# Moving a convolution's transposes from TensorE to DMA, and reordering the second row half, in a fused H3 and feed-forward kernel

## The chip, the cores and the metric

The kernel runs on one core of a Trainium2 chip, in one launch. The metric is the time of an execution in microseconds on the device, the median of several runs. A profile of one execution, taken by the hardware profiler, gives the durations.

## The reference, cut to what matters

The inputs are `q`, `k`, `v` and `x` of 2048 rows by 1024 channels; only `q` is used as x. The output is x plus a gated long convolution plus a feed-forward layer, both on the layer norm of x.

```python
xn = layernorm(q)
# long convolution, channel by channel
k_shift = sum of 4 taps of k           # causal, depthwise
kv = k_shift * v
y = irfft(rfft(kv padded to 2S) * rfft(ssm_k padded to 2S))[:S] + kv * ssm_D
conv = xn * y
# feed-forward
ffn = silu(xn @ w1) @ w2               # 1024 -> 3584 -> 1024
out = q + conv + ffn
```

## The kernel before, in words

**Precision and matmuls.** Every large operand is split into a high and a low fp16 part (`split`, L357: ACT writes the high part, then DVE writes the rest, `lo = src * scale - hi`). A product of 128 x 128 by 128 x 512 is then three matmuls (high by high, high by low, low by high).

**Feed-forward.** GEMM1 (lines L921 to L997) makes the hidden layer, transposed. The 28 column blocks of `w1` are taken as 14 pairs and the 2048 rows as two halves. Pairs 0 and 1 of the first half are plain. All the rest go as `units` (L962): a unit is one pair by one row half, done by seven products P1 to P7 of twelve matmuls each (a Strassen-Winograd scheme), each with its own left factor (B11, T1 and so on, in the `wo` buffers, made by `factors_w1`, L745) and its own moving operand (A11, S1 and so on, in the `x` places). The order is pairs 2 to 13 on the first half, then 0 to 13 on the second. In a unit the products stand as P7, P6, P2, P5, then P1 of the next unit, P3, P4, with PSUM banks evacuated by ACT and DVE (`evacuate`, L889).

Factors of pairs 2 to 13 are made once, used in the first half, written to DRAM (`spill_w1`, L786) and read back for the second half (`load_factors`, L797); pairs 0 and 1 are made for the second half alone, at the end of the first. The second half's seven moving operands lie in DRAM and come by seven transposing DMAs of 1 MB (`load_x`, L999; `X`, L326), each as soon as the first half's last unit has freed the place.

GEMM2 multiplies the hidden layer, written to DRAM and read back, by `w2`. The four pairs named in `PAIRS` (L43, 10 to 13) use the seven-product scheme again: their hidden values are combined and spilled by `quad` (L809) into `hsf`; the others are spilled by `blocks` (L851) into `hs`. Both write through two buffers `ht`.

**Convolution.** Eight groups g of 128 channels. `gate` (L1385) computes the taps and the product with v into `acc`, channels on partitions. `signal_parts` (L1436) prepares the transform's input for four parts t in the order 1, 3, 0, 2: TensorE transposes four 128 x 128 blocks of `acc` (fp32, against an identity) into the PSUM bank `px` (L1451), ACT and DVE split `px` into the first half of `hi` and `lo`; the filter `kf`, which comes from DRAM with time on partitions already, is split into the second half. `stage1` (L1459) multiplies by DFT constants, twelve matmuls per half part into PSUM banks `ps`. `to_spec` (L1496) moves sums and differences into `spec` and `tmp`. `forward` (L1511) does the butterflies on DVE, after all four parts; `product`, `inverse`, `result_parts` and `stage1_inv` (L1664, bank `py`) follow. `gated` (L1686) multiplies `py` by the normed rows `xg` into `yt`, and POOL adds `yt` to the output in DRAM (`G`, L331). Scales come from small matmuls (`norm`, L426) in the `px` bank.

**What sets the order.** All work is written as generators (streams), and `Order.run` (L165) takes, step by step, the operation that could start first by the kernel's own table of costs less a bias of its stream. The result is a fixed order on each engine and on SP's queue, which issues nearly all DMAs; each engine keeps its order and waits on semaphores. Ring buffers (L263) decide when a stream may go on.

Names on the engines in the profile: PE (TensorE), DVE (VectorE), ACT (ScalarE), POOL (GpSimd), SP (queue SPq). `split` shows as L347 (ACT) and L339 (DVE), loads as L324, transposing DMAs as L329.

Of the kernel before, what the change touches and what calls it, by code (L numbers as in the profile page):

```python
# [20 lines left out]
P = 128  # L21
# [15 lines left out]
WO = 6  # L37

# [4 lines left out]
PAIRS = (10, 11, 12, 13)  # L43
# [245 lines left out]
def h3_ffn_kernel(ctx, tc, x, kp, vs, fs, shift, dskip, w1, w2, cfwd, cinv, out):  # L289
# [78 lines left out]
    ws = {i: {n: dram.tile([P, 2, KH, len(n) * P], F16, name=f"ws{i}_{n[0]}") for n in FACTORS} for i in range(2, NP)}  # L368
# [48 lines left out]
    junk = rawa.tile([P, KH, 2 * P], BF16, name="junk")  # L417

# [48 lines left out]
    def ln_rows():  # L467
        for t0, n, bias in ((0, 2, 0.26), (2, 2, 0.17), (4, 4, 0.15), (8, 8, 0.03)):
# [5 lines left out]
            for t in order_in:  # L474
                yield flag["xt", t]
                xt, i = xts[t][0], slice(t - t0, t - t0 + 1)
                st = lnp.tile([P, 2, 6], F32, name="st", bufs=2)
# [5 lines left out]
                def moments():  # L483
                    nc.vector.bn_aggr(ag, st)
                    nc.vector.tensor_scalar(m[:, 0, i], ag[:, 0:1], -1.0, None, op0=MUL)
                    nc.vector.tensor_scalar(m[:, 3, i], ag[:, 1:2], 1e-5, None, op0=ADD)
                p = V(moments, m[:, 0, i], [st], us=0.5)
                p.writes.append(m[:, 3, i])
                yield p
            yield a_act(m[:, 4, :], m[:, 3, :], AF.Sqrt)  # L490
# [11 lines left out]
            for t in order_in:  # L502
                xt, i = xts[t][0], slice(t - t0, t - t0 + 1)
                yield V(lambda: nc.vector.tensor_scalar(xt, xt, m[:, 0, i], rstd[:, t:t + 1], op0=ADD, op1=MUL),
                        xt, [xt, m[:, 0, i], rstd[:, t:t + 1]], us=0.78)
                flag["xn", t].set()
# [238 lines left out]
    def factors_w1():  # L745
        for n, (kind, i) in enumerate(pairs):
# [50 lines left out]
    def load_factors():  # L797
        for i in range(2, NP):
# [153 lines left out]
    def product(n, i, sp, o, first=False):  # L952
# [6 lines left out]
        if i == NP - 1:  # L959
            xtok[sp][xname].set()  # L960

    def units():  # L962

        todo = [(i, 0) for i in range(2, NP)] + [(i, 1) for i in range(NP)]
# [3 lines left out]
        for n, (i, sp) in enumerate(todo):  # L968
            if sp == 1:
                flag["unit", i].set()  # L970
# [357 lines left out]
    def convolution(floor):  # L1328
# [12 lines left out]
        px_r, ps_r, py_r = ring("px", 1, ps_c), ring("ps", 2, ps_c), ring("py", 1, ps_c)  # L1341
        ctxs["nm"] = px_r
# [4 lines left out]
        def rest(floor):  # L1347
# [5 lines left out]
            for name, bufs in (("zh", 2), ("zl", 2), ("xg", 2), ("yt", 2)):  # L1353
# [6 lines left out]
        def loads():  # L1360
            for g in range(NG):
                for b in range(2):
# [4 lines left out]
                    if b == 0:  # L1367
                        yield kf_r.ready
                        kfs[g] = kf, _ = kf_r.tile([P, T2, 2, P], uses=4)
# [15 lines left out]
        def gate():  # L1385

            for g in range(NG):
# [8 lines left out]
                for a in range(2):  # L1396
                    yield hi_r.ready
                    j, tok = hi_r.tile([P, T2 // 2, 2, P], BF16)
                    yield a_act(j, kf[:, a * T2 // 2:(a + 1) * T2 // 2], AF.Square, total=ss[:, 4 + a:5 + a])
# [24 lines left out]
                yield from norm(px_r, ss[:, 0:6], (4, 2), then, ([sc[:, 0:4]], [flag["scales", g]]), 4.0)  # L1424
# [3 lines left out]
        def parts_tile(hr, lr):  # L1428

            two = []  # L1430
            for r in (hr, lr):
                yield lambda: r.ready() or flag["quads", 1]() and hts.ready()
                two.append((r if r.ready() else hts).tile([P, 2, 2 * 2 * P], F16))
            return two

        def signal_parts():  # L1436

            for g in range(NG):
# [4 lines left out]
                for t in TO:  # L1443
                    (hi, htok), (lo, ltok) = part[g, t] = yield from parts_tile(hi_r, lo_r)
                    yield px_r.ready
                    px, ptok = px_r.tile([P, 2, 2 * P])

                    def mm():
                        for i in range(2):
                            for b in range(2):  # L1450
                                nc.tensor.transpose(px[:, i, b * P:(b + 1) * P], acc[:, b, t + 4 * i, :], ident)  # L1451
# [359 lines left out]
```

## Time and profile before

| | |
|---|---|
| Median of 3 runs | 1280.16 us (1279.25 to 1280.81) |
| Span of the profiled execution | 1279.8 us, 0.36 us under the median |
| TensorE busy | 1244.7 us, 97% |
| VectorE busy | 1146.4 us, 90% |
| ScalarE busy | 725.5 us, 57% |
| GpSimd busy | 133.0 us, 10% |
| DMA on SP's queue | 258.54 MB, 63.6% of 16 engines' span |

How to read it: a group's row gives line, engine, operation, tile written <- tiles read, shape and count, then busy time and the mean of one, then the idle time of the engine just before and what ended it. A wait names the engine or DMA that came last by the profile; where that engine had long been done it was another. Matmuls overlap, so their pace is read from the distance between starts, not from the duration of one. A line of the timeline gives start, duration, engine, line, operation and count, and in brackets the idle time before it.

### The profile page before, as it was taken

How to read it: one execution, taken by the hardware profiler on the slowest of the kernel's cores; microseconds unless marked ns; L12 is line 12 of the kernel's file. 1: busy time of each engine (PE TensorE's matmuls, PEld its weight loads, DVE VectorE, ACT ScalarE, POOL GpSimd, SP SyncE). 2: the span in 40 equal slices, each digit the busy share in tenths (PEclk: the TensorE clock that was granted, in tenths of full speed). 3: DMA queues.
4: the chain of work that ended last, by engine and by line, in shares of the span. 5: the costliest groups of instructions: out<-in, count | busy, mean ns of one | idle time of the engine just before them, and what ended most of it. 6: DMA issues, size and time to landing. Idle time of an engine off the chain costs nothing. (4 is left out here: it accounts for less than half of the span.)

```text
span 1279.8 us, 17054 instructions
## 1 busy us (share of the span) xinstructions
PE 1244.7 (97%) x6082; PEld 604.2 (47%) x6082; DVE 1146.4 (90%) x1521; ACT 725.5 (57%) x1153; POOL 133.0 (10%) x141
## 2 busy tenths in 40 slices
PE   7899999989899999999999999999999999999997
PEld 6444444434344544445444544544454454445443
DVE  8999997889699969999899899899979989997991
ACT  6858896768566687559652632553253274445231
POOL 0000000000000020002010310210030030113223
PEclk9899999989999999999999999999999999999999
DMA  9447899889999899669995684598486487877766
GB/s 329 157 150 237 284 321 307 269 241 248 290 365 356 277 282 334 225 197 261 351 290 125 138 226 111 124 254 266 107 189 180 113 170 225 228 148 142 158 127 92
DMA packets 247988, 284.53 MB, mean 222 GB/s; under 512 B 43744, under 2 KB 162528, under 8 KB 246624
## 3 DMA queue, kind: packets, MB, share of 16 engines
q1 hardware_dynamic: 221168, 258.54, 63.6%
q0 software_dynamic: 26736, 24.92, 14.6%
q8 instruction: 47, 0.77, 0.2%
q14 instruction: 37, 0.30, 0.1%
HBM read 185.88 MB, written 98.57 MB: 222 GB/s over the span
## 5 line engine op out<-in xcount | busy, mean ns | idle before, releaser
L1054 PE MATMUL ff<-x,wo 128*128 128x512 f16 x864 | 327.4, 379 | 1.4 <-ACT hf L347 1.0
L1056 PE MATMUL ff<-x,wo 128*128 128x512 f16 x864 | 327.4, 379 | 0.0
L1055 PE MATMUL ff<-x,wo 128*128 128x512 f16 x864 | 327.4, 379 | 0.0
L926 PE MATMUL ff<-x,wo 128*128 128x512 f16 (+1 forms) x808 | 306.1, 379 | 8.6 <-ACT hf L347 3.8
L927 PE MATMUL ff<-x,wo 128*128 128x512 f16 (+1 forms) x808 | 306.0, 379 | 2.6 <-DVE x L339 2.6
L928 PE MATMUL ff<-x,wo 128*128 128x512 f16 (+1 forms) x808 | 306.0, 379 | 2.5 <-DVE wo L339 2.4
L336 DVE TENSOR_TENSOR spec<-spec 128x512 f32<-128x512 f32 (+2 forms) x256 | 260.6, 1053 | 2.8 <-DVE spec L336 0.5
L1056 PEld LDWEIGHTS <-wo 128*128 128x128 f16 x864 | 84.5, 98 | 101.9
L1055 PEld LDWEIGHTS <-wo 128*128 128x128 f16 x864 | 84.5, 98 | 100.8 <-issue 2.4
L1054 PEld LDWEIGHTS <-wo 128*128 128x128 f16 x864 | 85.4, 99 | 98.7
L928 PEld LDWEIGHTS <-wo 128*128 128x128 f16 x808 | 79.7, 99 | 101.8 <-issue 5.8
L926 PEld LDWEIGHTS <-wo 128*128 128x128 f16 x808 | 81.4, 101 | 92.2 <-ACT wo L347 3.4
L927 PEld LDWEIGHTS <-wo 128*128 128x128 f16 x808 | 79.7, 99 | 95.6 <-issue 9.1
L347 ACT ACTIVATE hf<-ff,invc 128x512 f32<-128x512 f32 x64 | 43.5, 680 | 118.9 <-PE ff L1056 86.8
L333 POOL DMA_DIRECT2D out<-yt x64 | 74.5, 1362 | 338.5 <-DVE yt L339 220.9
L333 POOL DMA_DIRECT2D out<-hf x63 | 57.4, 911 | 457.9 <-ACT hf L347 391.8
L336 DVE TENSOR_TENSOR tmp<-spec 128x2048 f32<-128x2048 f32 (+1 forms) x48 | 92.5, 1933 | 1.0
L347 ACT ACTIVATE spec<-spec 128x1024 bf16<-128x1024 f32 x32 | 33.8, 1055 | 86.1 <-DVE spec L336 86.0
L339 DVE SCALAR_TENSOR_TENSOR ht<-hf,wsc,ht 128x1024 f16<-128x1024 f32 (+1 forms) x56 | 67.3, 1204 | 13.7 <-ACT ht L347 13.7
L347 ACT ACTIVATE ht<-hf,wsc 128x1024 f16<-128x1024 f32 (+1 forms) x56 | 60.5, 1083 | 11.4 <-DMA hsfS<-ht 6.9
L339 DVE SCALAR_TENSOR_TENSOR wo<-raw,wsc,wo 128x512 f16<-128x512 f32 (+1 forms) x56 | 56.1, 1012 | 9.0 <-ACT wo L347 9.0
L339 DVE SCALAR_TENSOR_TENSOR acc<-kin,taps,acc 128x1024 f32<-128x1024 f32 x48 | 61.4, 1280 | 2.2 <-ACT acc L347 2.2
(181 smaller groups left out, 1750.1 us busy)
## 6 DMA issues: line engine op xcount, KB each, us to landing
wo<-hs SPq DMA_DIRECT2D x160, 256.0 KB, 3.6
hs<-ht SPq DMA_DIRECT2D x80, 256.0 KB, 5.6
out<-hf POOLq DMA_DIRECT2D x63, 256.0 KB, 4.5
raw<-in_w SPq DMA_DIRECT2D x28, 512.0 KB, 5.8
wraw<-in_w SPq DMA_DIRECT2D x24, 512.0 KB, 6.3
w2n<-in_w SPq DMA_DIRECT2D x24, 512.0 KB, 6.8
kin<-in_kp SPq DMA_DIRECT2D x16, 704.0 KB, 6.1
xt<-in_x SPq DMA_DIRECT2D x16, 512.0 KB, 7.4
```

Source lines behind the costliest of these rows:

```text
L333: return Op("POOL", 1.1, 3.0, lambda: nc.gpsimd.dma_start(o, i, accum_op=ADD), [i], [o], m, n)
L336: return V(lambda: nc.vector.tensor_tensor(o, a, b, op=op), o, [a, b], **k)
L339: return V(lambda: nc.vector.scalar_tensor_tensor(o, a, s, b, op0=op0, op1=op1), o, [a, b] + ([] if isinstance(s, float) else [s]), **k)
L347: nc.scalar.activation(o, i, func, scale=scale, **kw)
L926: nc.tensor.matmul(o, w[:, 0, k], xf[:, :, k, 0], start=first and k == 0, stop=False, **kw)
L927: nc.tensor.matmul(o, w[:, 0, k], xf[:, :, k, 1], start=False, stop=False, **kw)
L928: nc.tensor.matmul(o, w[:, 1, k], xf[:, :, k, 0], start=False, stop=last and k == KH - 1, **kw)
L1054: nc.tensor.matmul(po, hx[:, n, 0, :], wc[:, n, 0, :], start=first and n == 0, stop=False, **kw)
L1055: nc.tensor.matmul(po, hx[:, n, 0, :], wc[:, n, 1, :], start=False, stop=False, **kw)
L1056: nc.tensor.matmul(po, hx[:, n, 1, :], wc[:, n, 0, :], start=False, stop=last and n == 3, **kw)
```

## The change

Seven things are changed together.

1. The convolution's signal is split while channels are on the partitions, into a new buffer `cm` (one of it), and the two fp16 halves are transposed by two DMAs of 128 KB for each part, 64 in all, on SP. The TensorE transposes and the bank `px` are gone. `hi` and `lo` are laid out by signal or filter, then b, then i, and stage 1's moving operand takes four runs of 128. The filter's layout in DRAM changes to match.
2. Of the PSUM banks of the convolution, stage 1 has three (`ps`) in place of two, and the inverse keeps one (`py`), which the small scale matmuls now share.
3. The differences of the even parts are kept one place lower in `spec`, so that the two butterflies that read only odd parts come first and wait only for these; `to_spec` of an even part waits for one part of the group before, not two.
4. The second row half takes pair 13 first, then 0 to 12. Pair 13's factors stay in their buffers: five spills and five reloads are left out.
5. `PAIRS` are 8 to 11 in place of 10 to 13.
6. The gate is written into `xg` itself, of which there are four, and `yt` is gone.
7. In the layer norm the constant 1e-5 is added once for a group of rows; a copy stands in the place of each row's addition. (Two new lists, `ON_ACT` and `APPLY`, are empty, and so the lines under them do nothing.)

```diff
+PSB = 3
+XGB = 4
+CMB = 1
-PAIRS = (10, 11, 12, 13)
+PAIRS = (8, 9, 10, 11)
+UNITS = [[*range(2, NP)], [NP - 1, 0, 1, *range(2, NP - 1)]]
...
             def part(names, src):
                 spill = keep[names] is not None
-                o, tok = yield from w_place(len(names), 1 + spill)
+                both = i == NP - 1
+                o, tok = yield from w_place(len(names), 1 + spill + both)
                 yield from split(o[:, 0], o[:, 1], src, wsc[:, i, 0:1])
                 factors_there(sp, i, names, o, tok)
+                if both:
+                    factors_there(1, i, names, o, tok)
...
-        todo = [(i, 0) for i in range(2, NP)] + [(i, 1) for i in range(NP)]
+        todo = [(i, sp) for sp in range(2) for i in UNITS[sp]]
...
-        px_r, ps_r, py_r = ring("px", 1, ps_c), ring("ps", 2, ps_c), ring("py", 1, ps_c)
-        ctxs["nm"] = px_r
+        ps_r, py_r = ring("ps", PSB, ps_c), ring("py", 4 - PSB, ps_c)
+        cm_r = ring("cm", CMB)
+        ctxs["nm"] = py_r
...
                 for t in TO:
+                    yield cm_r.ready
+                    cm, ctok = cm_r.tile([P, 2, 2, 2, P], F16, 2)
+                    yield from split(cm[:, 0], cm[:, 1], acc[:, :, t::4, :], sc[:, 0:1])
                     (hi, htok), (lo, ltok) = part[g, t] = yield from parts_tile(hi_r, lo_r)
-                    yield px_r.ready
-                    px, ptok = px_r.tile([P, 2, 2 * P])
-
-                    def mm():
-                        for i in range(2):
-                            for b in range(2):
-                                nc.tensor.transpose(px[:, i, b * P:(b + 1) * P], acc[:, b, t + 4 * i, :], ident)
-                    yield T(mm, px, [acc[:, :, t::4, :]], 0.45, m=2.0)
-                    flag["part", g, t].n = 2
-                    f = kf[:, t:t + 5:4].rearrange("p i b w -> p i (b w)")
-                    add(split(hi[:, :, 0:2 * P], lo[:, :, 0:2 * P], px, sc[:, 0:1], (ptok, flag["part", g, t])), CB)
-                    add(split(hi[:, :, 2 * P:], lo[:, :, 2 * P:], f, sc[:, 1:2], (ktok, flag["part", g, t])), CB)
+                    flag["part", g, t].n = 3
+                    add(split(hi[:, 1], lo[:, 1], kf[:, :, t::4, :], sc[:, 1:2], (ktok, flag["part", g, t])), CB)
+                    for q, o in enumerate((hi, lo)):
+                        yield X(o[:, 0].rearrange("p b i w -> p (b i) w"), cm[:, q].rearrange("p b i w -> p (b i w)"))
+                        ctok.set()
+                        flag["part", g, t].set()
...
                 yield flag["taken", g - 1, t]
-                if t % 2 == 0:
-                    yield flag["taken", g - 1, t + 1]
...
+            yield flag["spec", g, 1]
             yield v_tt(R2(5, 2), R2(8, 1), I2(8, 1), ADD)
             yield v_tt(I2(5, 2), I2(8, 1), R2(8, 1), SUB)
             yield v_tt(pair(R(8), R(9)), pair(R(5), I(5)), pair(I(7), R(7)), ADD)
             yield v_tt(pair(I(8), I(9)), pair(I(5), I(7)), pair(R(7), R(5)), SUB)
+            yield flag["spec", g, 0]
...
-            flat = [q.rearrange("p b i w -> p (b i w)") for q in (yt, py, xg)]
-            yield v_stt(flat[0], flat[1], sc[:, 5:6], flat[2], MUL, MUL)
+            flat = [q.rearrange("p b i w -> p (b i w)") for q in (py, xg)]
+            yield v_stt(flat[1], flat[0], sc[:, 5:6], flat[1], MUL, MUL)
```

More of the change, by code (lines that the diff above doesn't have):

```diff
@@ L797, in load_factors @@
     def load_factors():
-        for i in range(2, NP):
+        for i in UNITS[1][3:]:
             for names in FACTORS:
@@ L969, in units @@
             if sp == 1:
-                flag["unit", i].set()
+                flag["unit", n - len(UNITS[0])].set()
                 flag["room", 1].set()
@@ L1352, in rest @@
             rb = late_w.enter_context(tc.tile_pool(name="rb", bufs=1, side="right"))
-            for name, bufs in (("zh", 2), ("zl", 2), ("xg", 2), ("yt", 2)):
+            for name, bufs in (("zh", 2), ("zl", 2), ("xg", XGB)):
                 more[name] = ring(name, bufs, rb)
@@ L1423, in then, with parts_tile @@
                     nc.vector.tensor_scalar(sc[:, 2:4], e, 2.0 ** 64, None, op0=MUL)
-                yield from norm(px_r, ss[:, 0:6], (4, 2), then, ([sc[:, 0:4]], [flag["scales", g]]), 4.0)
+                yield from norm(py_r, ss[:, 0:6], (4, 2), then, ([sc[:, 0:4]], [flag["scales", g]]), 4.0)
         CB = 0.03
-        def parts_tile(hr, lr):
+        def parts_tile(hr, lr, shape=(P, 2, 2, 2, P)):
             two = []
@@ L1432, in parts_tile @@
                 yield lambda: r.ready() or flag["quads", 1]() and hts.ready()
-                two.append((r if r.ready() else hts).tile([P, 2, 2 * 2 * P], F16))
+                two.append((r if r.ready() else hts).tile(shape, F16))
             return two
@@ L1591, in then @@
                 nc.vector.tensor_tensor(sc[:, 5:6], sc[:, 5:6], sc[:, 3:4], op=MUL)
-            yield from norm(px_r, ss[:, 8:12], (4,), then, ([sc[:, 4:6]], [flag["un", g], sss[g][1]]), 3.0)
+            yield from norm(py_r, ss[:, 8:12], (4,), then, ([sc[:, 4:6]], [flag["un", g], sss[g][1]]), 3.0)
         def inverse(g):
```

74 lines of the change are left out of this document (42 added, 32 removed).

## The prediction

> **What bounds the kernel now.** I read the page's busy shares first, then the table by stretches, the waits of TensorE, and the timeline around its longest wait.
>
> ```profile
> span 1279.8 us, 17054 instructions
> PE 1244.7 (97%) x6082; PEld 604.2 (47%) x6082; DVE 1146.4 (90%) x1521; ACT 725.5 (57%) x1153; POOL 133.0 (10%) x141
> ```
>
> TensorE (PE) is busy for 97% of the span, VectorE (DVE) for 90%. The stretches say where the missing 3% lies (columns: length, busy time and count by engine, granted clock, DMA share):
>
> ```profile
> 64.00:96.00 32.00, 32.00 (x151) 14.67 (x150) 29.54 (x60) 16.83 (x23) 0.00 (x0) 1.00 0.47 150
> 224.00:256.00 32.00, 30.64 (x144) 13.79 (x143) 25.68 (x42) 25.48 (x39) 0.00 (x0) 1.00 0.81 269
> 256.00:288.00 32.00, 28.40 (x123) 12.50 (x122) 28.15 (x46) 20.90 (x30) 0.00 (x0) 0.89 0.81 241
> 288.00:320.00 32.00, 31.63 (x152) 14.93 (x151) 29.30 (x41) 26.40 (x39) 0.00 (x0) 1.00 1.06 248
> 320.00:352.00 32.00, 27.51 (x119) 11.87 (x117) 22.25 (x24) 16.43 (x27) 0.76 (x1) 0.95 1.04 290
> 352.00:384.00 32.00, 30.28 (x141) 13.67 (x140) 31.00 (x29) 21.65 (x37) 0.00 (x0) 1.00 1.06 366
> 1184.00:1216.00 32.00, 32.00 (x150) 14.46 (x148) 31.52 (x33) 8.34 (x14) 6.87 (x8) 1.00 0.76 158
> ```
>
> A full stretch holds about 151 matmuls (first and last row). The five from 224 to 384 hold 144+123+152+119+141 = 679 where five full ones hold 755. That is the seam: first row half of GEMM1 ends, second begins. The 76 missing at 0.2157 us (below) are 16.4 us, and the sixteen short transposes counted among the 679 hide 16 x 0.11 = 1.7 us more: **the seam loses about 18 us**. Past 384 the busy column stays near full, so the rest of the program is TensorE's own work: removing matmuls there shortens the span one for one, and a new wait of TensorE lengthens it one for one.
>
> ```profile
> 262.09 0.38 PE L928 MATMUL ff<-x,wo 128*128 128x512 f16 x1
> ...
> 273.09 0.38 PE L928 MATMUL ff<-x,wo 128*128 128x512 f16 x1
> 276.37 0.61 PE L926 MATMUL ff<-x,wo 128*128 128x512 f16 x1 [2.90 <-ACT wo L347]
> ...
> 279.33 0.63 PE L927 MATMUL ff<-x,wo 128*128 128x512 f16 x1
> 279.75 0.63 PE L928 MATMUL ff<-x,wo 128*128 128x512 f16 x1
> ```
>
> 51 matmuls start between 262.09 and 273.09: 0.2157 us each, so a product of 12 takes 2.59 us. Then TensorE waits 2.9 us for a factor that ScalarE (ACT) was late with; by the order of instructions it is B11 of pair 13, the last pair of the first half. After that wait the matmuls start 0.42 us apart (279.33 to 279.75), half speed, and the stretch 256 to 288 shows what that costs: clock 0.89, 0.11 x 32 = 3.5 us. A long wait is paid again in clock.
>
> TensorE: Matmul & The Clock Gate, section "What's actually happening", of the Trainium skill says that an idle window of some 3.4 us halves the clock until some 3.4 us of work are done. The trace agrees roughly (3.3 us between the starts, 273.09 to 276.37); it would make waits below 3 us cost only themselves.
>
> The second long wait:
>
> ```profile
> 315.88 4.55 SPq L329 DMA_TRANSPOSE x<-xspS  x1
> 320.52 1.08 SPq L324 DMA_DIRECT2D hsfS<-ht  x2
> 321.69 6.12 SPq L329 DMA_TRANSPOSE x<-xspS  x1
> ```
> ```profile
> 324.64 0.72 ACT L347 ACTIVATE ht<-hf,wsc 128x512 f16<-128x512 f32 x1 [4.74 <-DMA hsfS<-ht]
> ```
> ```profile
> 327.48 0.52 PE L926 MATMUL ff<-x,wo 128*128 128x512 f16 x1 [2.89 <-ACT hf L347]
> ```
>
> Here ACT stands 4.74 us because its ht buffer is still being written out; that spill (hsfS, of a "quad" pair) was queued on SP behind a 1 MB transposing load that held SP's queue for 4.55 us. ACT's copy of a PSUM bank stands behind, and TensorE waits for that copy.
>
> **The change, part by part.** *PE transposes go.* 32 groups of four:
>
> ```profile
> 285.56 0.60 PE L1451 MATMUL px<-ident,acc 128*128 128x128 f32 x4
> 286.00 0.38 PE L926 MATMUL ff<-x,wo 128*128 128x512 f16 x1
> ```
>
> The next matmul starts 0.44 us after the group's first, so 32 x 0.44 = **14.1 us** leave a full TensorE. All other matmuls keep count and size; stage 1's moving operand becomes four runs of 128, as in GEMM1's products, which already go at 0.2157.
>
> *The split moves ahead of the transpose*, reading SBUF (acc) where it read PSUM (px):
>
> ```profile
> L339 DVE SCALAR_TENSOR_TENSOR lo<-kf,csc,hi 128x512 f16<-128x512 f32 x30 | 22.4, 745 | 0.3 <-ACT hi L347 0.3
> L339 DVE SCALAR_TENSOR_TENSOR lo<-px,csc,hi 128x512 f16<-128x512 f32 x30 | 22.4, 745 | 0.0
> L347 ACT ACTIVATE hi<-kf,csc 128x512 f16<-128x512 f32 x30 | 21.5, 717 | 2.7 <-DVE csc L1423 2.5
> L347 ACT ACTIVATE hi<-px,csc 128x512 f16<-128x512 f32 x30 | 20.4, 678 | 8.1 <-PE px L1451 8.0
> ```
>
> The kf rows are the same operation from SBUF: DVE 745 ns either way, ACT 39 ns more, 32 x 0.039 = 1.2 us on an engine 57% busy. Taken as nothing; were ACT the bound it would be 1.2 us.
>
> *64 DMA transposes of 128 KB come*, on SP. The only ones in the trace are seven of 1 MB (min/median/max ns on the queue; then us to landing):
>
> ```profile
> L329 SPq DMA_TRANSPOSE x<-xspS x4: 4546/6285/6567, 292.9 to 321.7; - x4
> L329 SPq DMA_TRANSPOSE x<-xspA x3: 4697/5480/5812, 283.0 to 329.1; - x3
> ...
> DMA to landing us min/median/max: 6.5/8.2/10.0
> ```
>
> An eighth is 0.57 to 0.82 us of the queue, 64 of them 36 to 52 us spread over some 800. Landing is bounded below by 0.57 plus what stays after the queue is free (6.5 - 4.55 = 2.0), 2.6 us, and above by the whole 10.0. The nearest rows of that size:
>
> ```profile
> hsfS<-ht SPq DMA_DIRECT2D x32, 256.0 KB, 4.0
> out<-yt POOLq DMA_DIRECT2D x64, 128.0 KB, 5.2
> xg<-in_x SPq DMA_DIRECT2D x36, 128.0 KB, 5.5
> ```
>
> I take 3.3 us for one and 4 us for a pair (hi, then lo), nearest to hsfS: whole rows, on SP. Who waits: counting matmuls in built order between a pair's issue and the first that reads it, 19 of the 32 pairs have over 10 us, two 6.5 and 7.1, and eleven (the third and fourth part of a group) only 5.2 to 5.8 us. At 4 us all are in time; loaded queues will make some late, and I put down **2 us** in all (from 0 to 11 x 4.8 = 53 us if every pair took 10). ACT also waits: its next split needs the one cm buffer read by both transposes, and PSUM copies of TensorE's banks queue behind it; the same lateness, the same bounds.
>
> *The seam.* Pair 13 now runs first in the second half with its factors kept, so pair 0's are wanted 18 us later than before, and five spills and five reloads go. The quads move from pairs 10-13 to 8-11, so the spill that held ACT at 324 isn't there. What stays are the seven 1 MB transposes. From the second half's P7 operand to its P5 operand SP holds four of them, two weight loads and four spills: 4 x 5.67 (the mean by the two rows above: (4.55 + 2 x 6.285 + 6.57 + 4.70 + 5.48 + 5.81) / 7) + 6 x 0.54 (row 320.52) + 2.5 to land (8.2 - 5.67) = 28.4 us; two spills ahead of the first add 1.1: 29.5. TensorE has nine products until it needs P5's operand, 23.3 us: 6.2 us late. P4's operand then costs two more transposes and two small ones, 12.8 us, against 10.3 us of matmuls (three products and twelve of stage 1): 2.5 more, and some 3 for half clock: 11.7. With the shortest transpose (4.55, landing 2.0 later) for all it is 18.2 + 3.2 + 2.0 + 1.1 - 23.3 = 1.2, and fewer spills between favour it; I take 6.5, the middle, and 1.5 for factor waits like these, whose margin in built order is as thin as before:
>
> ```profile
> PE ff L928 <- DVE wo L339: 2.4, 4, 0.7
> ```
>
> So the seam costs about 8 us (1 to 14) in place of 18: **10 gained**.
>
> *Odd butterflies first, three stage-1 PSUM banks, in-place gate.* These end waits of DVE and ACT, not of TensorE, whose own waits on stage 1 are
>
> ```profile
> PE ps L1485 <- ACT tmp L347: 1.5, 4, 0.6
> PE ps L1485 <- ACT spec L347: 0.7, 1, 0.7
> ```
>
> at most 2.2 us. DVE's waits for spec are larger (30.3 us, below) but DVE is not what ends the stages; they are the slack that lets it follow a shorter span. I count nothing (0 to 2.2).
>
> ```profile
> DVE spec L336 <- ACT spec L347: 30.3, 16, 3.9
> ```
>
> Sharing the inverse's bank with the scale sums, and four extra small adds in the layer norm: about 0, at most 1 us.
>
> **Sum**, against the profiled execution: 1279.8 - 14.1 - 10 + 2 = 1257.7. The median of the runs, 1280.16, is 0.36 above the span: **1258 us**.
>
> **Rivals.** (a) *The transposes land late, and it gets slower.* The place is the eleven tight pairs: stage 1 stands in front of everything else on TensorE. If a pair lands at the 1 MB median, 8.2, each is 8.2 - 5.2 = 3 us late: 33 us, 1257.7 - 2 + 33 = 1289. It turns slower than before when a pair takes more than about 5.2 + 25/11 = 7.5 us. For it: xg's 5.5 us for 128 KB, and ACT blocked for 4.74 us by a queue. Against it: that queue was full of 1 MB pieces, which is so only at the seam. Chance 0.13; in it, with 0.03, that a small transpose lands as late as the slowest large one, 10.0: eleven times 4.8 us, 1309.
>
> VectorE: DVE Perf Modes, section "The three transpose paths", of the Trainium skill speaks against the change: 390 ns for a 128x128 block on TensorE, 1309 ns by DMA, and it advises TensorE where PSUM will do. By that figure an estimate is 4 x 1.309 = 5.2 us for one transpose and 10.5 for a pair, 5.3 us late eleven times, 1314 us. The trace doesn't bear it out for large ones: 1 MB is 32 such blocks in 4.55 to 6.57 us, 0.14 to 0.21 each; no row shows a small one.
>
> (b) *The seam keeps its price*, as SP's chain of transposes takes the place of both waits: 1279.8 - 14.1 + 0.4 = 1266. For it: the 29.5 against 23.3 us. Against: 18 us needs two waits with half clock as well. 0.14.
>
> (c) *The seam closes*: transposes at 4.55, no wait: 1257.7 - 7 = 1251. 0.13.
>
> (d) *DVE becomes the bound*: its 1146.4 us are 91% of 1258, and its chain of a group (forward, product, inverse) is serial. The 14.1 us would then be given back: 1272. Against: its idle time before waiting on spec alone is 30 us. 0.05.
>
> Forecast (1253 to 1263): 0.55.
>
> **How the numbers follow.** Range 1248 to 1276: it takes in (b), (c) and (d) with their spread and leaves out (a) and the corners, about 0.18. A run can tell about 0.2% (2.6 us) from no change. Faster: forecast, (b), (c), (d) without their tails, 0.84; same 0.04; slower, (a) beyond its point, 0.12.
>
> **What would show it.** Right: no L1451 row; the five stretches over the seam hold some 45 matmuls more, with the clock near 1.00; the waits of TensorE name no stage-1 operand above 1 us; the 128 KB transposes take 0.6 to 0.8 us of SP and land in 3 to 4.5. Wrong: stage-1 matmuls waiting for DMA in the third and fourth part of each group (a); waits at the products P5 and P4 of the first second-half unit adding to over 10 us (b); TensorE waiting for DVE rows after 400 us (d).

## The result, and the profile after

The changed kernel took **1296.37 us**, the median of 4 runs (1293.55 to 1300.68), against 1279.99 for the kernel before in the same session: a ratio of 1.0131 (95% interval 1.0115 to 1.0146). It is 1.3% slower; 1258 was forecast.

The head of the page of after:

```profile
span 1293.0 us, 16973 instructions
PE 1235.7 (96%) x5954; PEld 590.2 (46%) x5954; DVE 1147.6 (89%) x1525; ACT 727.0 (56%) x1153; POOL 133.1 (10%) x141
```

TensorE (PE) has 128 matmuls less, the 32 x 4 transposes, and yet the span is 13.2 us longer. (The medians differ by 16.4 us: the profiled execution of after took 1294.81, 1.6 under its median. In the other runs a span is some 1.8 us under the execution's time, so the profiled execution of before was by estimate 1.4 above its median.) The same five stretches over the seam as in the prediction:

```profile
224.00:256.00 32.00, 30.90 (x145) 14.07 (x144) 24.46 (x33) 24.70 (x34) 0.95 (x1) 1.00 0.90 295
256.00:288.00 32.00, 29.79 (x139) 13.31 (x137) 31.76 (x47) 23.82 (x35) 0.00 (x0) 1.00 0.94 266
288.00:320.00 32.00, 27.78 (x120) 12.12 (x120) 22.34 (x34) 18.09 (x25) 0.00 (x0) 0.95 1.10 242
320.00:352.00 32.00, 29.87 (x121) 12.61 (x122) 15.91 (x20) 17.82 (x26) 0.00 (x0) 0.89 0.83 192
352.00:384.00 32.00, 32.00 (x150) 14.54 (x149) 21.93 (x23) 24.02 (x42) 0.76 (x1) 1.00 1.07 341
```

They hold 675 matmuls, none of them short, where before held 679 with 16 short ones. That is 12 long ones more, not 45, and the clock is still 0.95 and 0.89 in two of them. Look also at the third pair of numbers, VectorE (DVE): it is busy for 15.91 of 32 us.

The convolution phase. Stretches of before, then of after:

```profile
512.00:672.00 160.00, 160.00 (x782) 76.87 (x781) 152.57 (x190) 105.04 (x161) 13.13 (x13) 1.00 0.88 265
672.00:1200.00 528.00, 526.12 (x2602) 256.06 (x2601) 487.67 (x572) 223.24 (x386) 85.81 (x88) 1.00 0.69 171
```
```profile
512.00:672.00 160.00, 150.29 (x715) 70.29 (x714) 150.84 (x182) 100.60 (x150) 12.35 (x12) 0.99 0.91 263
672.00:1200.00 528.00, 515.69 (x2512) 245.30 (x2511) 500.12 (x588) 229.01 (x399) 84.27 (x86) 1.00 0.77 181
```

Here TensorE was full before and isn't any more: 9.7 and 10.4 us less busy. VectorE does more in the second stretch (500.12 of 528), which fits a backlog from the stages before.

To place the loss I took the start of each matmul and subtracted the time that all matmuls ahead of it in built order take at their full pace (0.2157 us for the long ones, 0.11 for a short transpose). The rest is what TensorE has lost so far. Its growth by stage, in us, a stage being named by TensorE's own matmul time (0 to 44 ends at 73 us of real time in after, 185 to 386 is 215 to 432, 386 to 607 runs to 667, 607 to 1190 to 1266; from 44 to 185 every kernel here loses the same 0.6 us):

| kernel | 0 to 44, start | 185 to 386, seam | 386 to 607, end of GEMM1 | 607 to 1190, convolution and GEMM2 |
|---|---|---|---|---|
| before | 24.7 | 18.7 | 0.4 | 4.3 |
| after | 29.1 | 16.6 | 13.5 | 16.1 |

Matmuls fell by 14.0 us as forecast, losses rose by 27.2: 4.4 at the start, 13.1 and 11.8 in the last two stages, 2.1 less at the seam.

### The profile page after: what moved, and what is told of

It is laid out like the page before. It is cut to its first block, busy times and chain, and to the rows that moved or that the text cites. A ratio compares the mean times of both kernels' runs of the same rounds, so it can differ in the third digit from the quotient of the medians.

```text
span 1293.0 us, 16973 instructions
## 1 busy us (share of the span) xinstructions
PE 1235.7 (96%) x5954; PEld 590.2 (46%) x5954; DVE 1147.6 (89%) x1525; ACT 727.0 (56%) x1153; POOL 133.1 (10%) x141
## 4 chain that ended last, share of the span: by engine, by line
PE 35%; DVE 29%; DMA 16%; issue 12%; ACT 4%; POOL 2%; SPq 1%; POOLq 0%; ACTq 0%; DVEq 0%
DVE spec L342 8%; PE ff L948 6%; PE ff L947 6%; PE ff L949 6%; PE ff L1075 4%; PE ff L1077 4%; PE ff L1076 4%; DVE tmp L342 3%; DMA wraw<-in_w 3%; DMA lo<-cm 3%; DVE x L345 2%; POOL out L339 2%; DVE ht L345 2%; DVE wo L345 2%; DVE acc L345 2%
## 5 line engine op out<-in xcount | busy, mean ns | idle before, releaser
L947 PE MATMUL ff<-x,wo 128*128 128x512 f16 (+1 forms) x808 | 306.2, 379 | 14.7 <-ACT hf L353 5.8
L339 POOL DMA_DIRECT2D out<-xg x40 | 45.2, 1284 | 300.2 <-DMA lo<-cm 136.3
```

What stands on the lines that cost most here:

```text
L339: return Op("POOL", 1.1, 3.0, lambda: nc.gpsimd.dma_start(o, i, accum_op=ADD), [i], [o], m, n)
L947: nc.tensor.matmul(o, w[:, 0, k], xf[:, :, k, 0], start=first and k == 0, stop=False, **kw)
```

## The experiments

**Theories.** (1) Every small transpose is dearer than foreseen, and ScalarE (ACT), which works in order, stands at the one `cm` buffer. (2) VectorE's chain of a group sets the pace of the convolution phase, so TensorE's removed work comes back as waits. (3) The layer norm's edit reordered the start. (4) At the seam the first group's small transposes stand in SP's queue behind 1 MB ones; VectorE starves and never catches up.

Runs named a_ start from after, b_ from before. In the runs "in the same order" every instruction keeps its place on its engine and only what it does is changed; in the others the order is made anew. All ratios are to the kernel before on the same chip, and a gain over after, which ran in another session, is given by medians and, where it differs by more than 1 us, by ratios too. The losses are those of one profiled execution: for a_g0pe (1288.28) and a_free_dve (1279.70) that was the longest of ten, which reached down to 1276.64 and 1271.45.

| run | median us | ratio (95%) | start | seam | end of GEMM1 | convolution and GEMM2 |
|---|---|---|---|---|---|---|
| b_drop | 1276.32 | 0.9963 (0.9948 to 0.9977) | 24.7 | 20.2 | 2.0 | 10.7 |
| b_drop_dve | 1269.41 | 0.9917 (0.9902 to 0.9932) | 25.0 | 19.8 | 1.5 | 3.3 |
| b_dve | 1277.70 | 0.9989 (0.9976 to 1.0002) | 23.9 | 16.3 | 0.5 | 3.7 |
| b_seam | 1278.99 | 0.9994 (0.9984 to 1.0003) | 24.9 | 10.2 | 1.6 | 8.0 |
| b_dma | 1314.05 | 1.0259 (1.0236 to 1.0283) | 25.1 | 38.9 | 8.6 | 22.0 |
| a_plain | 1287.66 | 1.0051 (1.0036 to 1.0066) | 29.3 | 13.8 | 12.9 | 13.2 |
| a_big | 1286.79 | 1.0043 (1.0026 to 1.0059) | 29.5 | 4.5 | 18.0 | 16.5 |
| a_free | 1279.71 | 0.9996 (0.9983 to 1.0009) | 29.0 | 4.0 | 14.7 | 14.5 |
| a_free_dve | 1275.72 | 0.9969 (0.9952 to 0.9985) | 29.8 | 5.2 | 13.6 | 12.0 |
| a_dve | 1291.22 | 1.0080 (1.0065 to 1.0095) | 30.5 | 16.1 | 16.6 | 8.4 |
| a_ln | 1294.31 | 1.0091 (1.0072 to 1.0110) | 23.7 | 27.9 | 7.9 | 17.7 |
| a_pe | 1289.86 | 1.0072 (1.0057 to 1.0087) | 29.8 | 11.9 | 10.6 | 4.7 |
| a_xc | 1288.22 | 1.0073 (1.0055 to 1.0091) | 29.4 | 16.0 | 12.5 | 11.8 |
| a_g0pe | 1283.26 | 1.0030 (1.0012 to 1.0049) | 29.5 | 12.4 | 5.0 | 20.5 |
| a_g0pe_xc | 1276.40 | 0.9968 (0.9956 to 0.9979) | 30.1 | 7.1 | 3.1 | 16.2 |
| a_g0pe_xc_ln | 1284.90 | 1.0034 (1.0012 to 1.0056) | 23.9 | 11.4 | 10.2 | 18.8 |
| a_eb10 | 1288.71 | 1.0070 (1.0051 to 1.0090) | 29.7 | 7.1 | 15.8 | 15.2 |
| a_eb15 | 1287.57 | 1.0064 (1.0044 to 1.0085) | 30.0 | 9.6 | 15.2 | 9.8 |

### Does less TensorE work shorten the span?

**b_drop.** Before, same order:

```diff
-                                nc.tensor.matmul(ps, cf[:, 0], lo[:, i], start=False, stop=False, **kw)
+                                if i:
+                                    nc.tensor.matmul(ps, cf[:, 0], lo[:, i], start=False, stop=False, **kw)
```

> The kernel before, every instruction in its old order, without the product of the constants' high part and lo in the first half of each stage-1 part (64 of 128x512, 64 x 0.2157 = 13.8 us of TensorE; that part of the transform is left out). The step on trial is the prediction's sentence that past 384 us removed matmuls shorten the span one for one, tested with almost the 14.1 us that the change removed and in the same places. If it holds: 1280.0 - 13.8 = 1266. If VectorE's serial chain of a group sets the pace of the convolution phase, TensorE gives most of it back as waits: 1275 to 1280.

13.8 us of matmuls are gone and the run is 4.7 us faster than the kernel before in its session (1280.99): a third. TensorE, full before, now waits (row of b_drop; before had 526.12 there with 2602 matmuls):

```profile
672.00:1200.00 528.00, 521.62 (x2575) 253.13 (x2574) 491.29 (x575) 223.92 (x390) 85.81 (x88) 1.00 0.69 172
```

**b_drop_dve** and its control **b_dve**: the edit of b_drop (only in the first) and, in `forward`,

```diff
-                yield v_stt(flat[0], flat[1], r, flat[2], MUL, ADD)
+                p = v_stt(flat[0], flat[1], r, flat[2], MUL, ADD)
+                cut = [f[:, :, 0:64] for f in flat]
+                p.emit = lambda cut=cut, r=r: nc.vector.scalar_tensor_tensor(cut[0], cut[1], r, cut[2], op0=MUL, op1=ADD)
+                yield p
```

> The kernel before, every instruction in its old order, without the 64 stage-1 matmuls of the run b_drop (13.8 us of TensorE) and with the 32 forward operations of VectorE shortened as in the run a_dve (30 us of VectorE); those parts of the transform are left out. b_drop alone gave 4.7 of 13.8 us. If VectorE is what took the other 9 back, as theory 2 has it: 1266 to 1268. If the fixed interleaving of the engines took them (ScalarE between the two, whatever VectorE does): 1272 to 1276.

> Control: the kernel before, same order, with the same 32 operations shortened, nothing else. There TensorE loses only 4.8 us past its 326th us of matmuls, so the shorter VectorE can give at most that: 1275 to 1280. If it gives as much as in b_drop_dve over b_drop (6.9 us) or more, VectorE bounds the kernel before too and TensorE's busy column misled: 1273 or less.

By the ratios b_drop gives 4.7 us, the shorter VectorE alone 1.4, which can't be told from nothing, and both together 10.6: 4.5 more than the two add up to. **The step "past 384 us removed matmuls shorten the span one for one" is shown false** for the kernel in its old order; in an order made for the smaller work it wasn't tried. About half of the 9.1 us given back in b_drop is VectorE's: by the three intervals the 4.5 us are uncertain by some 3. The row of b_drop_dve, 479.04 us of VectorE against 491.29, with TensorE full again:

```profile
672.00:1200.00 528.00, 526.78 (x2605) 256.31 (x2603) 479.04 (x580) 227.39 (x395) 87.90 (x91) 1.00 0.70 174
```

**b_seam.** Before with `UNITS`, kept factors and the new `PAIRS` alone, the lines of the change's diff.

> The kernel before with the pair order alone: pair 13 first in the second half with its factors kept, PAIRS 8 to 11, spills and reloads left out; the order made anew; transposes on TensorE as before. The prediction's seam step gives 1280 - 10 = 1270. If the seam's price is the 1 MB transposes on SP's queue in either order (rival b): 1280 within 4. TensorE's loss between its 246th and 326th us of matmuls says which: 13.2 us in the kernel before; the step foresaw about 3 to 6.

The seam's loss falls from 18.7 to 10.2, nearly the step's 18 to 8. The time hardly moves: the last stage's loss rises from 4.3 to 8.0, so the profiled span falls by 3.7 us (1279.8 to 1276.1), and the medians by only 1.2 (1280.15 to 1278.99), the rest being the spread of executions. My seam step was right for the order alone; that its gain reaches the end was not.

### What do the DMA transposes cost?

**b_dma.** Before with item 1 of the change alone (`cm`, two DMAs for a part, layout of `hi`, `lo`, `fs`).

> The kernel before with the first part of the change alone: signal split on channels, 64 transposing DMAs, hi and lo in the new layout; the order made anew; pairs, factors, banks, butterflies, gate and layer norm as before. The prediction's steps give 1280 - 14.1 + 2 = 1268. Theory 4 gives a first group that is late by 10 to 20 us and a time of 1285 to 1300, with TensorE's waits after 450 us up by 15 or more. If it comes out between 1272 and 1283, the seam's reordering and not the transposes carry the loss.

34 us slower than the kernel before, where the prediction's steps gave 1268; it is worse than I had expected on any theory. The seam's loss doubles, from 18.7 to 38.9. So the DMA transposes are bad by themselves, and the other six edits together win back about half: after is 16 us slower than before, b_dma 34.

**a_pe.** After with the transposes back on TensorE:

```diff
-        ps_r, py_r = ring("ps", PSB, ps_c), ring("py", 4 - PSB, ps_c)
+        px_r, ps_r, py_r = ring("px", 1, ps_c), ring("ps", 2, ps_c), ring("py", 1, ps_c)
...
-                    cm, ctok = cm_r.tile([P, 2, 2, 2, P], F16, 2)
-                    yield from split(cm[:, 0], cm[:, 1], acc[:, :, t::4, :], sc[:, 0:1])
+                    px, ptok = px_r.tile([P, 2, 2, P])
+                                nc.tensor.transpose(px[:, b, i, :], acc[:, b, t + 4 * i, :], ident)
+                    add(split(hi[:, 0], lo[:, 0], px, sc[:, 0:1], (ptok, flag["part", g, t])), CB)
...
-                        yield X(o[:, 0].rearrange("p b i w -> p (b i) w"), cm[:, q].rearrange("p b i w -> p (b i w)"))
```

> The kernel after with its transposes back on TensorE (with the bank px, two stage-1 banks), all else as after; the order made anew; 14.1 us of TensorE more. If the DMA transposes carry the loss (theories 1 and 4), it is faster than after in spite of that work: 1270 to 1285. If the other edits carry it, it is slower: 1296 + 14 = 1310, or at least not below 1296.

6.5 us faster than after (7.6 by the ratios) in spite of 14 us more of TensorE's work. In the last stage it loses 4.7 where after loses 16.1, so 11.4 us of waits stand there in place of a part of the transposes' 14.0. That the one became the other is not shown, since the order was made anew. It missed the range that I had expected, 1270 to 1285.

**a_plain, a_big, a_free.** After, same order; the 64 small transposes, the seven large ones, or both as plain copies (the edit for the small ones; in `load_x` it is the same):

```diff
-                        yield X(o[:, 0].rearrange("p b i w -> p (b i) w"), cm[:, q].rearrange("p b i w -> p (b i w)"))
+                        p = X(o[:, 0].rearrange("p b i w -> p (b i) w"), cm[:, q].rearrange("p b i w -> p (b i w)"))
+                        p.emit = lambda o=o, q=q, cm=cm: nc.sync.dma_start(o[:, 0].rearrange("p b i w -> p (b i w)"), cm[:, q].rearrange("p b i w -> p (b i w)"))
+                        yield p
```

> The kernel after, same instructions in the same order, but the 64 transposing DMAs of 128 KB are plain copies of the same 128 KB (so the signal isn't transposed). Theory 1, the transposes' price on SP's queue and their late landing, through ScalarE that stands 36.5 us in order at the one cm buffer, cost the time lost after 400 us: the waits at cm fall to below 10 us, the queue time of one to some 0.5 us, and the time to about 1296.4 - 15 = 1281 or less. Theory 2, VectorE's chain sets the pace whatever the transposes do: the time stays above 1292.

> The kernel after, same instructions in the same order, but the seven transposing loads of 1 MB for the second row half are plain loads of the same bytes (so those operands aren't transposed). Theory 4: at the seam the first group's small transposes stand on SP's queue behind the 1 MB ones (4.6 to 6.8 us each), ScalarE stands at the one cm buffer, VectorE idles 35 us between 300 and 400 us where it idled 13, and as VectorE is some 95% busy from there to 1220 us it never catches up. Then VectorE's idle time there falls below 20, the first group's fourth energy square comes some 10 to 20 us earlier than 441, and the time falls by 10 to 15: 1281 to 1286. Rival: the lateness is made later, by the order itself and by each group's own transposes: VectorE's idle time falls but the time by under 5 us, above 1291.

> The kernel after, same instructions in the same order, with both earlier edits at once: the 64 small and the seven 1 MB transposing DMAs are all plain copies of the same bytes (nothing that they carry is transposed). The small ones alone gave 8.7 us, the large ones alone 9.6. If the two are separate causes: 1296.4 - 18.3 = 1278. If both measure the same thing, the first group's start at the seam: about 1285. If the whole loss against my forecast were the transposes' price, 1260 to 1265.

8.7 us, 9.6 us and 16.7 us by the medians: nearly separate (10.2, 11.3 and 17.3 by the ratios: they overlap by some 4). **All transposing by DMA together costs about 17 us.** Not all of it belongs to the 38 between forecast and result: the seven 1 MB transposes stand in before as well, and the forecast had 6.5 us for them. No run has these plain without the small ones, so the two shares aren't told apart. a_plain lies between what theories 1 and 2 asked for, and its waits at `cm` fell less than theory 1 had it (36.5 to 25.7 us). The place is the seam. SP's queue in after, then ScalarE:

```profile
312.79 5.20 SPq L335 DMA_TRANSPOSE x<-xspS  x1
318.08 1.22 SPq L335 DMA_TRANSPOSE hi<-cm  x1
319.39 1.22 SPq L335 DMA_TRANSPOSE lo<-cm  x1
320.70 4.62 SPq L335 DMA_TRANSPOSE x<-xspS  x1
```
```profile
321.85 0.72 ACT L353 ACTIVATE cm<-acc,csc 128x512 f16<-128x512 f32 x1 [3.05 <-DMA lo<-cm]
```

The first part of the first group was in `cm` by 303 us (its ACT half starts at 300.5, its DVE half at 302.1). Its transposes are issued at 318.08, behind three 1 MB ones, and the next part enters `cm` only at 321.85. The last copy of stage 1's results into the first group's `spec` starts 33 us later than in before (before, then after):

```profile
338.57 0.69 DVE L336 TENSOR_TENSOR spec<-spec,ps 128x512 f32<-128x512 f32 x1 [1.89 <-ACT spec L347]
```
```profile
371.48 0.69 DVE L342 TENSOR_TENSOR spec<-spec,ps 128x512 f32<-128x512 f32 x1 [1.32 <-ACT spec L353]
```

In a_big, in the same order but with plain 1 MB loads, the first small transpose is issued 15.9 us earlier than in after, and that last copy starts 11.8 us earlier:

```profile
302.19 2.23 SPq L335 DMA_TRANSPOSE hi<-cm  x1
```
```profile
359.65 0.69 DVE L342 TENSOR_TENSOR spec<-spec,ps 128x512 f32<-128x512 f32 x1 [1.32 <-ACT spec L353]
```

What VectorE could do between 300 and 400 us is the third pair of numbers, here of before, after, b_dma, a_big, a_free, b_seam and a_g0pe_xc:

```profile
300.00:400.00 100.00, 93.42 (x428) 42.42 (x427) 86.06 (x99) 65.33 (x106) 0.76 (x1) 0.98 1.03 312
```
```profile
300.00:400.00 100.00, 93.91 (x410) 41.10 (x409) 65.00 (x71) 61.68 (x100) 0.76 (x1) 0.95 1.01 279
```
```profile
300.00:400.00 100.00, 81.28 (x329) 33.85 (x328) 64.49 (x70) 54.90 (x86) 0.76 (x1) 0.88 1.06 283
```
```profile
300.00:400.00 100.00, 100.00 (x465) 45.23 (x464) 76.47 (x81) 71.54 (x115) 0.76 (x1) 1.00 0.94 308
```
```profile
300.00:400.00 100.00, 100.00 (x465) 45.34 (x463) 76.28 (x82) 71.54 (x116) 0.76 (x1) 1.00 0.90 312
```
```profile
300.00:400.00 100.00, 100.00 (x475) 46.58 (x473) 87.94 (x100) 68.97 (x110) 0.76 (x1) 1.00 0.98 291
```
```profile
300.00:400.00 100.00, 98.17 (x465) 45.58 (x464) 87.58 (x106) 67.94 (x108) 0.76 (x1) 1.00 0.94 281
```

In these rows it is 86 to 88 us where TensorE transposes the first group, 64 to 65 with the DMAs behind transposing 1 MB loads, 76 behind plain ones. (The other runs spread more: 83 to 94 with TensorE, 63 to 68 behind transposing loads.) Theory 4's mechanism is shown: the queue makes the first group late, and VectorE idle. It isn't all of the lateness: a_free, with no transposing at all, still has 76 and not 86. That VectorE "never catches up" is shown only in part, since a_big wins 12 us at the seam and gives some 5 of them back in the stages behind it.

**a_g0pe, a_xc, a_g0pe_xc.** After with the first group's transposes on TensorE (in the `py` bank), with the measured price of a transposing DMA in the plan, and with both; order made anew:

```diff
+                    if g < 1:
+                        px, ptok = py_r.tile([P, 2, 2, P])
...
+                                    nc.tensor.transpose(px[:, b, i, :], acc[:, b, t + 4 * i, :], ident)
...
+                        continue
...
-        return Op("SP", 0.6, 0.1, lambda: nc.sync.dma_start(o, i, transpose=True), [i], [o], m, 1.2 * n)
+        big = n > 500e3
+        return Op("SP", 5.4 if big else 1.25, 2.6, lambda: nc.sync.dma_start(o, i, transpose=True), [i], [o], m, 1.2 * n)
```

> The kernel after with the first group alone transposed by TensorE (py bank), the planner's prices as in after; the order made anew. Theory 4 (the first group behind the 1 MB transposes): most of the 20 us of a_g0pe_xc, 1276 to 1283, and the first group's fourth energy square at 410 to 420. If the price in the plan was what counted there: 1287 or more.

> The kernel after with the measured price of transposing DMAs in the plan alone (1.25 us for 128 KB, 5.4 for 1 MB, landing 2.6 us later), all transposes of the signal by DMA; the order made anew. Theory 4: the first group still queues behind the 1 MB ones, 1286 to 1296, its fourth energy square after 435. If a right price is enough: 1280 or less.

> The kernel after with two edits, the order made anew: the first group's four parts are transposed by TensorE as in the kernel before (through the py bank, 4 x 0.44 = 1.8 us), so no small transpose stands in the seam's queue; and the planner's price of a transposing DMA is 1.25 us of SP for 128 KB and 5.4 us for 1 MB, 2.6 us more to landing, in place of 0.6 and 0.1. Theory 4: the first group is ready some 20 us earlier, VectorE's idle time from 300 to 400 us falls below 20, and 10 to 18 us come back: 1278 to 1286. Theory 1 (each group's transposes cost by their lateness at cm): the price in the plan removes most of that, 1283 to 1288. Rival, VectorE's serial chain sets the pace in every group: above 1290.

An energy square is a pass of ScalarE that sums the squares of one of four parts of a group's `product`; the group's inverse can only be scaled after the fourth. a_g0pe gives 13.1 us, a_xc 8.2 (its first group stays late: fourth energy square at 443 us, 413 in a_g0pe), both together 20.0: **1276.40, faster than after and, by 0.3%, than before** (0.9956 to 0.9979). How much of each figure is the edit's and how much the new order's isn't shown: a_g0pe_xc with one bias of the planner changed, a_eb10 below, took 1288.71.

### The start, the pace of VectorE, and what is left

**a_ln** and **a_g0pe_xc_ln** restore the layer norm:

```diff
-                    nc.vector.tensor_copy(m[:, 3, i], ag[:, 1:2])
+                    nc.vector.tensor_scalar(m[:, 3, i], ag[:, 1:2], 1e-5, None, op0=ADD)
-            yield V(lambda: nc.vector.tensor_scalar(m[:, 3, :], m[:, 3, :], 1e-5, None, op0=ADD), m[:, 3, :], [m[:, 3, :]], us=0.15)
```

> The kernel after with the layer norm as before: 1e-5 added row by row, no copy and no one addition for the group. Theory 3, this edit reordered the start, where TensorE loses 4.4 us more than before by 44 us of its matmuls: 1292, and the stretch up to 64 us reads as in the kernel before. Rival: the start's loss has another source (the pair order or the factors kept), and the time stays at 1296 within 2. All later order is made anew from the planner's clock, so some 3 us either way may come from there; the first 64 us decide.

> The run a_g0pe_xc (first group transposed by TensorE, transposes priced as measured) with the layer norm as before as well. By theory 3 the start loses 5 us less than in that run: 1276.4 - 5 = 1271. If the order made anew gives it back later, as in the run a_ln, where 3 of 5 us were given back: 1274 to 1281.

First 64 us of before, after and a_ln:

```profile
0.00:64.00 64.00, 51.44 (x302) 34.79 (x303) 57.44 (x143) 50.06 (x92) 0.69 (x6) 0.92 0.69 243
```
```profile
0.00:64.00 64.00, 48.26 (x281) 33.67 (x282) 55.46 (x146) 46.56 (x87) 0.70 (x6) 0.89 0.69 241
```
```profile
0.00:64.00 64.00, 51.13 (x306) 34.55 (x307) 57.20 (x143) 50.03 (x92) 0.69 (x6) 0.92 0.70 243
```

Theory 3 is shown for the start: 5.4 us come back there (29.1 to 23.7). a_ln then loses 11 us more at the seam and is 2.1 us faster than after by the medians, 5.1 by the ratios, neither clear of after's own runs (1293.55 to 1300.68); a_g0pe_xc_ln is 8.5 us slower than a_g0pe_xc, outside what I had expected. A gain at the start need not be a gain at the end when the whole order behind it is made anew.

**a_dve** and **a_free_dve**: the shortened forward in after and in a_free, same order.

> The kernel after, same instructions in the same order, but the last four operations of each forward butterfly work on 64 of 512 columns (32 operations shorter by about 0.93 us, 30 us of VectorE in all; the rest of those columns is left as it was). Theory 2, VectorE's chain of a group sets the pace from about 700 to 1220 us: the 12 us that TensorE lost there come back, 1284, and ScalarE's 47 us at zh shrink by 20 or more. Theory 1, ScalarE and the transposes are late by themselves: at most 3 us, 1293.

> The run a_free (after, same order, all transposing DMAs as plain copies, so nothing that they carry is transposed) with the 32 forward operations of VectorE shortened by 30 us in all as in a_dve. If VectorE takes most of the 22 us that a_free leaves above the forecast: 1265 to 1270. If the interleaving does, whatever VectorE's work: 1275 to 1279.

5.2 (6.5 by the ratios) and 4.0 us from 30 us less of VectorE; a_dve lies between what the two theories asked for. In a_dve the last stage's loss halves (16.1 to 8.4), so VectorE takes part; the end of GEMM1 doesn't gain. Theory 2 as the one cause falls for after.

**a_eb10, a_eb15**: a_g0pe_xc with `EB`, the bias of evacuations, at 0.10 and 0.15 for 0.06.

> The run a_g0pe_xc with the planner's precedence for evacuations of TensorE's banks raised from 0.06 to 0.10 us, the order made anew. If TensorE's waits past its 386th us of matmuls are evacuations queued behind convolution work on ScalarE and VectorE, they shrink by 5 or more of 19 us: 1271 or less. If VectorE's full share of the phase makes them whatever stands first: 1273 to 1280.

> The same with the precedence at 0.15 us. If order is the cause, at least as good as at 0.10. If VectorE is full, the convolution comes later for it, and the time rises: 1278 to 1288.

Both are about 12 us slower than a_g0pe_xc: precedence for evacuations isn't the cure, and a_eb10 lies outside both of its expected ranges. They also show how far the time moves when only the order changes: runs whose order was made anew can't be told apart within some 12 us by their times alone. How much of after's 16 us is a poor order is open: a_xc is after's own instructions in another order and 8.2 us faster, and no run orders before anew by itself.

Two places in after where waits sit, first ScalarE at `cm`, and TensorE behind it:

```profile
555.03 0.72 ACT L353 ACTIVATE cm<-acc,csc 128x512 f16<-128x512 f32 x1 [4.90 <-DMA lo<-cm]
```
```profile
556.29 0.38 PE L947 MATMUL ff<-x,wo 128*128 128x512 f16 x1 [3.28 <-ACT hf L353]
```

and at `zh`, where ScalarE stands for VectorE's inverse with stage 1's `tmp` copy behind it:

```profile
727.96 2.19 ACT L353 ACTIVATE zh<-spec,csc 128x1024 f16<-128x1024 f32 x2 [10.15 <-DVE spec L345]
```
```profile
730.67 0.38 PE L1506 MATMUL ps<-hi,cfw 128*128 128x512 f16 x1 [1.94 <-ACT tmp L353]
```

In a_free TensorE's longest wait has ScalarE standing for a load of `w2`, with the evacuation of `hf` behind it; TensorE stands 5.4 us for that (a line of the timeline, and TensorE's waits):

```profile
630.44 1.15 ACT L353 ACTIVATE x<-w2n,tau 128x1024 f16<-128x1024 f32 x1 [6.31 <-DMA w2n<-in_w]
```
```profile
PE ff L1077 <- ACT hf L353: 6.5, 3, 5.4
```

**Open:** a_free still stands 22 us above the forecast. 4 of them are the start, 4 go with a shorter VectorE. The rest lie in the last two stages; the longest waits there have another engine or a DMA ahead of ScalarE, which keeps its order. No run takes them all away, none gives `cm` a second buffer or the small transposes another queue, and no single cause is shown.

## Why the prediction was wrong, point by point

- **"Removing matmuls there shortens the span one for one"**: the step that failed. The 14.0 us left as counted, but b_drop shows that such a cut is worth a third in the old order, and after waits 11.4 us more in the last stage than a_pe. I read a TensorE 97% busy as the only bound past 384 us, and VectorE's idle time as slack; from 512 to 672 us of before VectorE is busy 152.57 of 160. My rival (d), VectorE becomes the bound, had 0.05; its mechanism is part of the truth, its 1272 far too good.
- **The small transposes.** Queue time 0.57 to 0.82 us foreseen, 1.2 measured. Landing of one: 3.3 us foreseen, 3.8 measured (rows below). Landing of a pair: 4 foreseen, by estimate 5.1 measured, as `lo` is issued 1.3 us after `hi` (318.08 and 319.39 above). That is just inside the 5.2 to 5.8 us that the eleven tight pairs had, and they were not the trouble:

```profile
PE ps L1506 <- ACT tmp L353: 6.4, 3, 2.6
PE ps L1506 <- DMA hi<-cm: 2.3, 2, 2.0
PE ps L1507 <- DMA lo<-cm: 1.7, 3, 0.9
```

 TensorE waited 4.0 us for DMAs in stage 1 (2 foreseen), and more, 6.4, for ScalarE's copies of its banks. What failed is the sentence on `cm`, "the same lateness, the same bounds". It left out the queue at the one place where I had shown it full. I had the row of ScalarE standing 4.74 us behind a 1 MB transpose and used it only to dismiss rival (a), "so only at the seam"; the first group of the convolution is at the seam. Measured in all:

```profile
ACT cm L353 <- DMA lo<-cm: 36.5, 16, 6.8
```

- **Rival (a)**, slower by late transposes, 0.13: right in direction, wrong in place. It was not the end of each group but the head of the first, with ScalarE and VectorE between. That its 1289 is near 1296 is luck: its eleven times 3 us didn't occur. VectorE: DVE Perf Modes, section "Rules for kernel authors", of the Trainium skill advises TensorE here, and by the 1309 ns a block of 128x128 of its section "The three transpose paths" I had worked out an estimate of 5.2 us a transpose. The trace disagrees with that estimate (1.2 us of queue, 3.8 to landing). On the advice the runs are divided: a_pe, all on TensorE, is 6.5 us faster than after, but a_g0pe_xc, with 28 of 32 parts by DMA, is 13.5 us faster than a_pe.
- **The seam, 18 to 8**: measured 18.7 to 10.2 in b_seam, where the order stands alone. In after 16.6, in b_dma 38.9: the first group's transposes lengthen the same queue. I had worked out the two steps each alone, and the transposes undid most of the seam's gain. (In the sum for P4's operand, two transposes and two small ones are 12.4 us, not 12.8; that moves the seam by 0.2. Rival (b)'s 1266 leaves out the sum's 2 us for late pairs.)
- **Layer norm "at most 1 us"**: 4.4 us at the start. The extra operation itself is short (0.17 us). In the order made anew ScalarE has other work ahead of its first copy of a transposed bank, which starts at 13.69 us where before had it at 11.02, and TensorE waits longer for ScalarE's next copies (before, then after; over the first 73 us):

```profile
PE ft L521 <- ACT xt L347: 2.1, 1, 2.1
```
```profile
PE ft L539 <- ACT xt L353: 5.8, 2, 3.8
```

- **Split from SBUF, gate in place, banks, butterflies at nothing**: no run tells these apart. a_pe has the gate in place and the early butterflies (it goes back to the split from PSUM and to two stage-1 banks), and the new pair order too; that it is 9.5 us slower than before, 5 of them at the start, speaks against a gain from these.

## What to carry to other kernels

When two engines are over 90% busy in the same stage, test "this engine's removed work is removed time" before adding it to a sum: a cut of about the same size in the old kernel, in the old order, showed a third of it. Ask of every new DMA what stands ahead of it in its queue at its worst place, not on average, and which in-order engine stands still behind a single buffer until it lands. An edit that is good alone can lose its gain to another that fills the same queue, so work out two such edits together; and an order that is made anew can spend a gain far from where it was made.

## What the runs showed of the hardware

A transposing DMA of 128 KB between SBUF buffers, in after (min/median/max ns on SP's queue, and us to landing for all of them):

```profile
L335 SPq DMA_TRANSPOSE lo<-cm x31: 1188/1218/2187, 319.4 to 1163.2; - x31
L335 SPq DMA_TRANSPOSE hi<-cm x30: 1189/1258/3647, 318.1 to 1161.9; - x30
DMA to landing us min/median/max: 2.4/3.8/8.3
```

It holds the queue for 1.2 us in the median, about a quarter of what 1 MB holds it (4.6 to 6.8 us), so an eighth of the size is not an eighth of the price. As plain copies (a_plain):

```profile
L1474 SPq DMA_DIRECT2D lo<-cm x31: 464/546/1012, 318.6 to 1156.5; - x31
L1474 SPq DMA_DIRECT2D hi<-cm x30: 464/485/933, 317.9 to 1155.7; - x30
DMA to landing us min/median/max: 1.9/3.6/7.5
```

Landing is nearly the same, 3.6 us; what transposing adds at this size is time on the queue. For 1 MB that is far more: plain, five of the seven hold the queue for 0.33 to 0.53 us in a_big (the other two for 1.1 and 3.0), where transposing they hold it for 4.6 to 6.8 in after.
